# Attention's weights and maxima in steps of four heads instead of two, in a state-space convolution mixed with segmented attention

## The chip, the core and the metric

The kernel runs on one core of a Trainium2 chip. The metric is the device time of one execution in microseconds (us). Five engines of the core matter here and run side by side, each with its own queue of instructions in fixed order: TensorE (PE, with the weight loads shown apart as PEld), VectorE (DVE), ScalarE (ACT), GpSimd (POOL) and SyncE (SP), which here only issues DMAs.

## What is computed

Two branches read the same `x` of 2048 rows by 448 columns and are mixed by a gate per row. Branch A is a long convolution whose kernel is a sum of 256 damped oscillations per column; branch B is attention with 16 heads of 28 columns, in 4 segments of 512 rows, causal inside a segment, with a running memory across segments.

```python
def _A_ref(u, ...):
    P = jnp.exp((A * dt[:, None])[:, :, None] * pos[None, None, :])
    K = 2.0 * jnp.einsum("dn,dnl->dl", C, P).real
    y = jnp.fft.irfft(jnp.fft.rfft(u_t, L2) * jnp.fft.rfft(K, L2)[None], L2)[:, :, :L]
    return y + u * D_skip[None, None, :]

def _B_ref(x, wq, wk, wv, wo, beta):
    for s in range(N):                       # 4 segments of 512 rows
        logits = jnp.einsum("bhqd,bhkd->bhqk", qs, ks) * scale + mask
        a_dot = jnp.einsum("bhqk,bhkd->bhqd", _softmax(logits, axis=-1), vs)
        num = jnp.einsum("bhld,bhde->bhle", pq, M)
        den = jnp.einsum("bhld,bhd->bhl", pq, z)[..., None] + 1e-6
        outs.append(g * num / den + (1.0 - g) * a_dot)
        ...
    return o @ wo

g = _sigmoid((x * gate_w).sum(-1, keepdims=True))
return g * a + (1 - g) * b
```

## The kernel before

The work has two halves. The first (`first_half`, to about 444 us) makes the convolution's kernel and, woven into it, the projections q, k and v; q and k go to DRAM, split into a high and a low part. The change does not touch it. The second half (`second_half`, line 1206) does everything that the change touches.

**Units.** Attention is cut into 16 units: 4 segments times 4 groups of 4 heads. In SBUF the four heads of a unit lie in four blocks of 32 partitions, so that a product of one head uses 32 of TensorE's 128 rows: one row tile (`tile_position=(32 * h, 0)`). For each unit there are three steps.

- `maxima(i)` (line 974) computes the plain logits, queries by keys, and takes each row's maximum on DVE (line 994, tile `jk` with the result in `mx`). It then transposes the maxima on PE and stores them, negated, into an unused row of q by a DMA of the POOL queue (lines 1001 to 1005), so that the exponent needs no further subtraction.
- `weigh(i)` (line 1008) computes the logits again, keys by queries, in three products for each head (high by high, low by high, high by low), and ACT writes their exponentials to `PT` (line 1024). POOL then blanks the triangle above the diagonal (line 1035).
- `values(i)` (line 1037) multiplies `PT` by v on PE (tile `ps_pv`), and ACT copies the result to `pvs` (line 1055).

**Places.** Of the 512 by 512 logits of a head only the causal part is computed, in four blocks of 512, 384, 256 and 128 columns. `PLACES` (line 972) packs them into three places of one PSUM bank each: place 0 has 512 columns, place 1 has 384 and 128, place 2 has 256. In `maxima` the tile `ps_a` is written from `ku,qu`, in `weigh` from `qu,ku`.

**Steps of two heads.** `STEPS` and `MSTEPS` list six steps a unit: each place, for one half `hp` of the heads. A step takes one PSUM buffer `ps_a` of two banks, one bank for each of its two heads. The maxima of a step use the half of the heads that the weights beside it do not use.

**Three buffers.** PSUM holds three buffers `ps_a` (six of its eight banks), handed out in turn, one bank `ps_m` and one bank `ps_pv`. The convolution, the transform of its kernel and the last stage take buffers from the same three: `transform_k` two for each step (products `kb,s1k`, copied out by ACT and DVE as `gs`), `convolve` one for each step (`gk,cf`, read by ACT as `ks`; `gu,cf`, read by DVE as `pr`; `pr,cb`, read by ACT as `bs`), `finish.last` one (`bt,fc`, read by DVE).

**Order.** All products stand on PE in the order in which the program writes them. That order is written by hand in `second_half`. A first loop of 8 steps runs `transform_k` with the maxima of unit 0 and the first of unit 1 between; four more steps of unit 1 follow. Then comes a round for each unit `i`, in six turns `r`: a step of `maxima(i + 2)` (`ahead`) and a step of `weigh(i)` (`w`); at `r` 0 and 1 the tail of `maxima(i + 1)` (`behind`); at `r` 1 `values(i - 1)`; at the other turns a step of a segment's end (`seg_end`: reciprocals by way of DRAM, products `r,sel`, then four projections `wo,pvs`, 8 records each, into the one bank `ps_m`); and from round 1 to 12 some 1.15 steps of the convolution a turn. Rounds 14 and 15 have no maxima left and run `last` instead. The order on DVE and ACT is made when the program is built, from a schedule.

**Unread products.** `turn_over(n)` (line 1223) runs n products of 128x512 in bf16 into `ps_pv` that nobody reads (tile `wz`). Round 0 has three at each turn, the other rounds 1, 3 and 3 at the turns 3, 4 and 5 (`WARM`), the loop ahead of the rounds 4 times three, and the steps with `last` one each: 143 in all.

## Time and profile before

| What | us |
|---|---|
| runs of the kernel (median of 3) | 850.76 (848.26 to 857.52) |
| profiled execution, first to last instruction | 850.4 |
| transform of the convolution's kernel, maxima of units 0 and 1 | 444 to 476 |
| round 0 | 476 to 489.8 |
| rounds 1 to 12 | 489.8 to 750.8 |
| round 13 | 750.8 to 788 |
| rounds 14 and 15 | 788 to 833 |
| last projection and stores | 833 to 850.4 |

The borders of the rounds are the starts of each round's first exponential on ACT, less 1 us. The profile gives no time of its own for the profiled execution beside its span of 850.4 us; that lies 0.4 us under the median of the runs, so what is worked out against the span can be set beside the median. In the views, "idle before" with an arrow names what ended an engine's wait; `32*128 32x512` is a product on 32 rows with 512 columns, and a product in plain fp32 has two records.

### The profile page before, as it was taken

How to read it: one execution, taken by the hardware profiler on the slowest of the kernel's cores; microseconds unless marked ns; L12 is line 12 of the kernel's file. 1: busy time of each engine (PE TensorE's matmuls, PEld its weight loads, DVE VectorE, ACT ScalarE, POOL GpSimd, SP SyncE). 2: the span in 40 equal slices, each digit the busy share in tenths (PEclk: the TensorE clock that was granted, in tenths of full speed). 3: DMA queues.
4: the chain of work that ended last, by engine and by line, in shares of the span. 5: the costliest groups of instructions: out<-in, count | busy, mean ns of one | idle time of the engine just before them, and what ended most of it. 6: DMA issues, size and time to landing. Idle time of an engine off the chain costs nothing.

```text
span 850.4 us, 19021 instructions
## 1 busy us (share of the span) xinstructions
PE 750.1 (88%) x7608; PEld 405.1 (48%) x7608; DVE 582.0 (68%) x1143; ACT 538.6 (63%) x638; POOL 171.8 (20%) x217
## 2 busy tenths in 40 slices
PE   1686987998879989899988999989997998988997
PEld 1363655764546655566643444434443444343443
DVE  8878678767788676876687765656565757563474
ACT  4867889799998989898863255554453444521320
POOL 5314111011110111001110121341115113331110
PEclk9589999999999989799999899999999999979899
DMA  9347853325642346314558967667466645654872
GB/s 248 91 108 237 247 186 112 99 91 172 197 143 85 104 153 200 132 46 149 178 202 349 349 221 235 204 220 233 118 219 220 194 152 182 210 205 152 223 231 97
DMA packets 88290, 152.98 MB, mean 180 GB/s; under 512 B 20626, under 2 KB 57162, under 8 KB 88154
## 3 DMA queue, kind: packets, MB, share of 16 engines
q1 hardware_dynamic: 79130, 140.83, 51.7%
q10 hardware_dynamic: 7424, 9.18, 3.1%
q0 software_dynamic: 1648, 1.76, 0.8%
q8 instruction: 60, 0.98, 0.5%
q14 instruction: 28, 0.23, 0.1%
HBM read 90.87 MB, written 60.63 MB: 178 GB/s over the span
## 4 chain that ended last, share of the span: by engine, by line
PE 54%; ACT 16%; DVE 15%; DMA 7%; issue 6%; POOL 1%; SPq 1%; ACTq 0%; DVEq 0%; POOLq 0%
PE ps_a L1379 19%; PE ps_m L1379 17%; PE ps_pv L1379 8%; ACT cs L1344 7%; PE ps_arg L1379 5%; PE ps_k L1379 3%; DVE jk L994 3%; DVE Y L397 2%; ACT L1344 2%; PE ps_m L1382 2%; DVE Y L398 1%; DVE X L393 1%; DMA xt<-in_A_u 1%; ACT EX L1344 1%; DMA ident<-in_c_id 1%
## 5 line engine op out<-in xcount | busy, mean ns | idle before, releaser
L994 DVE CUSTOM_DVE_ANT_0 jk<-ps_a,mk 128x512 f32<-128x512 f32 (+3 forms) x256 | 124.9, 488 | 71.0 <-PE ps_a L1379 63.7
L1024 ACT ACTIVATE PT<-ps_a 128x1024 f32<-128x1024 f32 (+1 forms) x96 | 84.5, 881 | 118.6 <-PE ps_a L1379 112.0
L359 POOL TENSOR_TENSOR EX<-EX,cab 128x1024 f32<-128x1024 f32 x28 | 53.5, 1913 | 309.1 <-ACT EX L1344 244.8
L1344 ACT ACTIVATE cs<-ps_arg 128x1024 f32<-128x1024 f32 x111 | 107.3, 1021 | 0.6 <-DVE Y L398 0.3
L1379 PE MATMUL ps_m<-xh,w 112*128 112x512 f32 x256 | 92.9, 412 | 0.4 <-DVE lo L765 0.4
L1379 PE MATMUL ps_a<-qu,ku 32*128 32x512 f32 (+3 forms) x768 | 89.3, 353 | 1.7 <-DVE mx L994 1.4
L1035 POOL TENSOR_SCALAR_AFFINE_SELECT PT<-PT 128x256 f32<-128x256 f32 (+1 forms) x96 | 46.5, 485 | 206.5 <-ACT PT L1024 206.4
L393 DVE TENSOR_TENSOR X<-EX,cs 128x1024 f32<-128x1024 f32 x56 | 68.3, 1220 | 25.4 <-ACT cs L1344 25.4
L1379 PE MATMUL ps_k<-Y,X 128*32 128x64 f32 x3584 | 64.1, 226 | 9.0 <-DVE Y L398 8.8
L1379 PEld LDWEIGHTS ps_k<-Y,X 128*32 128x32 f32 x3584 | 54.9, 113 | 35.2 <-DVE Y L398 16.1
L397 DVE TENSOR_TENSOR Y<-EY,cs 128x1024 f32<-128x1024 f32 x56 | 70.0, 1250 | 0.0
L1379 PEld LDWEIGHTS ps_a<-qu,ku 32*128 32x128 f32 x768 | 62.4, 194 | 12.4 <-DVE mx L994 4.7
L1344 ACT ACTIVATE cs<-cs,bhp 128x1024 f32<-128x1024 f32 x56 | 64.5, 1151 | 1.8
L399 DVE SCALAR_TENSOR_TENSOR Y<-EY,cs 128x512 f32<-128x512 f32 x56 | 41.0, 732 | 31.2 <-ACT cs L1344 29.1
L1344 ACT ACTIVATE EY<-ps_arg 128x1024 f32<-128x1024 f32 x52 | 53.1, 1031 | 11.1 <-PE ps_arg L1379 10.1
L1379 PEld LDWEIGHTS ps_m<-xh,w 112*128 112x128 f32 x256 | 48.0, 188 | 19.7 <-issue 7.6
L1379 PE MATMUL ps_a<-ku,qu 32*128 32x512 f32 (+3 forms) x256 | 46.0, 394 | 12.3 <-DVE mx L994 9.9
L1379 PE MATMUL ps_arg<-ct,lh 64*128 64x512 bf16 x224 | 43.6, 387 | 9.0 <-ACT cs L1344 5.7
L1379 PE MATMUL ps_m<-xl,w 112*128 112x512 f32 x128 | 50.3, 393 | 0.0
L1379 PEld LDWEIGHTS ps_a<-ku,qu 32*128 32x128 f32 x256 | 22.2, 189 | 58.7 <-DVE mx L994 27.0
L1379 PEld LDWEIGHTS <-lh 64*128 64x128 bf16 x392 | 22.2, 95 | 53.4 <-issue 39.8
L606 DVE TENSOR_TENSOR pr<-ps_a,ks 128x896 f32<-128x896 f32 x32 | 34.8, 1087 | 17.7 <-PE ps_a L1379 17.0
(212 smaller groups left out, 1395.3 us busy)
## 6 DMA issues: line engine op xcount, KB each, us to landing
w<-WD SPq DMA_DIRECT2D x32, 448.0 KB, 4.7
qu<-QD SPq DMA_DIRECT2D x16, 512.0 KB
ku<-KD SPq DMA_DIRECT2D x16, 512.0 KB
GU<-gs SPq DMA_DIRECT2D x32, 224.0 KB, 2.5
GK<-gs SPq DMA_DIRECT2D x8, 896.0 KB, 5.1
gk<-GK SPq DMA_DIRECT2D x32, 224.0 KB, 4.7
gu<-GU SPq DMA_DIRECT2D x32, 224.0 KB, 3.7
BB<-bs ACTq DMA_DIRECT2D x16, 448.0 KB, 2.6
```

Of the source, the lines that this page charges most:

```text
L359: nc.gpsimd.tensor_tensor(o, o, cab, ALU.mult)
L393: v.tensor_tensor(X, ex, t[:, :, 0], ALU.mult)
L397: v.tensor_tensor(Y[:, :, :, :32], lo, y[:, :, :, ::-1], ALU.mult)
L398: v.tensor_tensor(Y[:, 0, :, 32:], ey[:, :, 32:], y[:, 0], ALU.mult)
L399: v.scalar_tensor_tensor(Y[:, 1, :, 32:], ey[:, :, 32:], -1.0, y[:, 1], ALU.mult, ALU.mult)
L606: nc.vector.tensor_tensor(pr[c], pt, ks.pop(c), ALU.mult)
L994: v.tensor_tensor_reduce(junk[:, :n], pt[:, x, o : o + n], k.mk[:, SEG - n :], 1.0, -3e38, ALU.add, ALU.max, mx[:, 3 - t, h : h + 1],)
L1024: nc.scalar.activation(PT[:, 2 * hp : 2 * hp + 2, 512 * b : 512 * b + n], pt[:, :, :n], AF.Exp, scale=SCALE)
L1035: nc.gpsimd.affine_select(sl, sl, pat, ALU.is_ge, 0.0, base=0, channel_multiplier=-1)
L1344: x = op(*args, **kw)
L1379: tc.keep_in_program_order(nc.tensor.matmul(*args, **kw))
L1382: tc.keep_in_program_order(nc.tensor.transpose(*args))
```

## The change

`weigh` and `maxima` no longer work on two heads in a step but on four: a step takes two `ps_a` buffers and issues, for its place, the products of all four heads, one head on each row tile. A unit then has three steps of weights and three of maxima instead of six and six. In the rounds they go by turns: the weights at `r` 0, 2 and 4, the maxima of the unit two ahead at `r` 1, 3 and 5. The list of maxima on the other half of the heads (`MSTEPS`) goes, and so do the unread products of rounds 1 to 15 (`WARM`); those of round 0 and of `last` stay, and of the loop ahead of the rounds two of the four remain, since that loop has two steps instead of four. Everything else, each product's size and number and all DMAs, is as before.

```diff
-    STEPS = [(b, hp) for b in range(3) for hp in range(2)]
-    MSTEPS = [(b, 1 - hp) for b, hp in STEPS]
...
     def maxima(i):
-        for b, hp in MSTEPS:
-            pt = k.ps("a")
-            for t, o, n in PLACES[b]:
+        for place in PLACES:
+            pts = [k.ps("a") for _ in range(2)]
+            for t, o, n in place:
                 qt = 3 - t
-                for x in range(2):
-                    h = 2 * hp + x
+                for h in range(4):
                     r = slice(32 * h, 32 * h + 32)
                     k.mm(
-                        pt[:, x, o : o + n], q[r, 0, 128 * qt : 128 * qt + 128], kk[r, 0, :n],
+                        pts[h // 2][:, h % 2, o : o + n], q[r, 0, 128 * qt : 128 * qt + 128], kk[r, 0, :n],
...
     def weigh(i):
-        for b, hp in STEPS:
-            pt = k.ps("a")
-            for kt, o, n in PLACES[b]:
+        for b, place in enumerate(PLACES):
+            pts = [k.ps("a") for _ in range(2)]
+            for kt, o, n in place:
                 for a, (x, y) in enumerate(((0, 0), (1, 0), (0, 1))):
-                    for z in range(2):
-                        h = 2 * hp + z
+                    for h in range(4):
...
-        for _ in range((0, 1, 2, 1, 2, 1, 1, 0)[r]):
+        if r in (1, 2, 4, 5, 6):
             step(ms[0])
-        if r >= 6:
+        if r == 7:
             step(ms[1])
...
-    for r in range(4):
+    for r in range(2):
         turn_over(3)
         step(ms[1])
...
             if i == 0:
                 turn_over(3)
-                step(w)
-                step(ahead)
-            else:
-                if r in WARM:
-                    turn_over(WARM[r])
-                step(ahead)
-                step(w)
+            step(ahead if r % 2 else w)
...
-WARM = {3: 1, 4: 3, 5: 3}
```

How the products stand on PE in the middle of a plain round, before (round 2, from its place 1 on). `gk,cf` and `gu,cf` are the convolution's, `ku,qu` the maxima's, `qu,ku` the weights':

```order
L1379 MATMUL ps_a<-gk,cf 128x448 x2
L1379 MATMUL ps_a<-ku,qu 128x384 x2
L1379 MATMUL ps_a<-ku,qu 128x128 x2
L1379 MATMUL ps_a<-qu,ku 128x384 x6
L1379 MATMUL ps_a<-qu,ku 128x128 x6
L1379 MATMUL ps_a<-gu,cf 128x448 x2
L1379 LDWEIGHTS wz
L1379 MATMUL ps_pv<-wz 128x512
L1379 MATMUL ps_a<-ku,qu 128x384 x2
L1379 MATMUL ps_a<-ku,qu 128x128 x2
L1379 MATMUL ps_a<-qu,ku 128x384 x6
L1379 MATMUL ps_a<-qu,ku 128x128 x6
```

And after (round 3, the same place and the one behind it):

```order
L1369 MATMUL ps_a<-gu,cf 128x448 x2
L1369 MATMUL ps_a<-gk,cf 128x448 x2
L1369 MATMUL ps_a<-qu,ku 128x384 x12
L1369 MATMUL ps_a<-qu,ku 128x128 x12
L1369 MATMUL ps_a<-gu,cf 128x448 x2
L1369 MATMUL ps_a<-ku,qu 128x384 x4
L1369 MATMUL ps_a<-ku,qu 128x128 x4
L1369 MATMUL ps_a<-pr,cb 64x448 x4
L1369 MATMUL ps_a<-qu,ku 128x256 x12
L1369 MATMUL ps_a<-gk,cf 128x448 x2
L1369 MATMUL ps_a<-ku,qu 128x256 x4
L1369 MATMUL ps_a<-gu,cf 128x448 x2
```

The maxima moved away from the weights that stood right behind them, by one or two steps of the convolution, and the unread products between the steps are gone.

On DVE the reductions of a place stand in one run of four heads. Of the same stretch before, one place of two heads, then another, with the convolution's `pr` between:

```order
L994 ISA jk,mx<-ps_a,mk 128x384
L994 ISA mx 128x1
L994 ISA jk,mx<-ps_a,mk 128x128
L994 ISA mx 128x1
L994 ISA jk,mx<-ps_a,mk 128x128
L994 ISA mx 128x1
L606 TENSOR_TENSOR pr<-ps_a,ks 128x896
L994 ISA jk,mx<-ps_a,mk 128x384
L994 ISA mx 128x1
L994 ISA jk,mx<-ps_a,mk 128x384
```

And after:

```order
L606 TENSOR_TENSOR pr<-ps_a,ks 128x896 x2
L991 ISA jk,mx<-ps_a,mk 128x384
L991 ISA mx 128x1
L991 ISA jk,mx<-ps_a,mk 128x384
L991 ISA mx 128x1
L991 ISA jk,mx<-ps_a,mk 128x128
L991 ISA mx 128x1
L991 ISA jk,mx<-ps_a,mk 128x128
L991 ISA mx 128x1
L991 ISA jk,mx<-ps_a,mk 128x384
L991 ISA mx 128x1
```

Two of `pr` moved together ahead of the place, and the eight reductions of a place 1 follow one another.

In the last rounds PE has the weights beside `last` (`bt,fc`), before (round 15):

```order
L1379 MATMUL ps_a<-bt,fc 64x448 x4
L1379 LDWEIGHTS wz
L1379 MATMUL ps_pv<-wz 128x512
L1379 MATMUL ps_a<-qu,ku 128x384 x6
L1379 MATMUL ps_a<-qu,ku 128x128 x6
L1379 MATMUL ps_a<-bt,fc 64x448 x4
L1379 LDWEIGHTS wz
L1379 MATMUL ps_pv<-wz 128x512
L1379 LDWEIGHTS wz
L1379 MATMUL ps_pv<-wz 128x512
L1379 MATMUL ps_a<-qu,ku 128x384 x6
L1379 MATMUL ps_a<-qu,ku 128x128 x6
```

And after:

```order
L1369 MATMUL ps_a<-bt,fc 64x448 x4
L1369 LDWEIGHTS wz
L1369 MATMUL ps_pv<-wz 128x512
L1369 MATMUL ps_a<-qu,ku 128x384 x12
L1369 MATMUL ps_a<-qu,ku 128x128 x12
L1369 MATMUL ps_a<-bt,fc 64x448 x4
L1369 LDWEIGHTS wz
L1369 MATMUL ps_pv<-wz 128x512
L1369 MATMUL ps_m<-pvs,den 128x512
```

Here the two bursts of weights became one, and one unread product a step is left. (The line numbers of the changed file are 3 lower inside `attend` and 10 lower behind `second_half`.)

28 lines of the change are left out of this document (15 added, 13 removed).

## Prediction

> **What bounds the kernel now.** I read the stages first, then the chain of waits inside a round, then single rows. One execution by stage (the columns are length, busy time of PE, PEld, DVE, ACT and POOL, granted PE clock, share of the DMA engines, GB/s):
>
> ```profile
> 476.00:489.80 13.80, 13.25 (x87) 6.82 (x87) 8.84 (x36) 5.79 (x7) 2.85 (x7) 0.75 0.97 350
> 489.80:542.30 52.50, 51.36 (x417) 23.42 (x415) 31.82 (x107) 29.94 (x36) 10.58 (x22) 1.00 0.67 208
> 542.30:615.20 72.90, 68.66 (x465) 30.37 (x464) 41.22 (x123) 32.57 (x40) 19.50 (x34) 0.98 0.62 201
> 615.20:633.70 18.50, 18.50 (x150) 8.60 (x152) 11.83 (x37) 10.31 (x13) 3.82 (x8) 1.00 0.63 202
> 633.70:750.80 117.10, 106.77 (x739) 47.88 (x733) 71.60 (x204) 51.87 (x64) 38.68 (x61) 0.94 0.57 187
> 788.00:833.00 45.00, 44.72 (x279) 18.45 (x279) 26.08 (x37) 12.56 (x16) 7.04 (x14) 0.93 0.80 226
> ```
>
> In the plain rounds 1 to 3 and 7 (second and fourth row; 17.5 us each on average, and 18.5) PE is busy all the time, DVE and ACT some 60%. The chain of waits over round 7 stays on PE almost wholly, a fifth of it in the bank `ps_pv`, where the unread products go too:
>
> ```profile
> by line: PE ps_a L1379 71.8%; PE ps_pv L1379 21.7%; ACT bs L619 4.9%; PE ps_m L1382 2.8%; PE ps_m L1379 1.2%; issue 0.1%
> ```
>
> So these rounds are PE's own length. They are also well packed:
>
> ```profile
> 586.05 1.02 PE L1379 MATMUL ps_a<-gk,cf 64*128 64x448 f32 x4
> 587.01 0.50 PE L1379 MATMUL ps_a<-ku,qu 32*128 32x512 f32 x2
> 587.01 0.96 PE L1379 MATMUL ps_a<-qu,ku 32*128 32x512 f32 x6
> 587.90 1.40 PE L1379 MATMUL ps_m<-wo,pvs 128*128 128x448 f32 x3
> ```
>
> Two products of the maxima start in the same 10 ns as the first two of the weights, because they use the other two row tiles, and all eight give way to the next work after 0.89 us: the time of the six alone. Before the change the maxima are nearly free on PE, and four row tiles already work at once for a third of the time.
>
> **The change, part by part.**
>
> *Four heads in a burst.* Twelve products on four tiles are not in this trace, so I bound them: 0.89 us if four tiles take the time of two, 1.78 us if not. The nearest row is the convolution kernel's transform, on four tiles:
>
> ```profile
> 451.19 2.00 PE L1379 MATMUL ps_a<-kb,s1k 32*128 32x448 f32 x16
> ```
>
> 16 records of 448 columns in 2.00 us with the tail is four at a time; I take 0.89, and 1.1 and 0.6 for places 1 and 2. The maxima now stand alone and pay for themselves, about 0.4 us a burst. A round then has 2.6 + 1.2 = 3.8 us of these products against 2 x 2.6 = 5.2 before, a gain of 1.4 us of PE (a loss of 1.2 at the other end).
>
> *Unread products.* Three take 0.75 us of PE's time, start to next start:
>
> ```profile
> 578.14 0.82 PE L1379 MATMUL ps_pv<-wz 128*128 128x512 bf16 x3
> 578.89 0.38 PE L1379 MATMUL ps_a<-ku,qu 32*128 32x256 f32 x2
> ```
>
> Seven in a round go, 1.8 us; with the loop ahead it is 111 of 143. So PE's own work in a plain round falls from 17.5 to about 14.3 us. What it waits for next are the buffers.
>
> *Two buffers a step, of three.* The durations that decide (ACT's exponential of two heads, DVE's reductions of one head by place, the convolution's readers):
>
> ```profile
> L1024 ACT ACTIVATE PT<-ps_a 128x1024 f32<-128x1024 f32 x64 | 65.4, 1024 | 73.9 <-PE ps_a L1379 67.3 <-ACT bs L619 3.2 <-DMA gk<-GK 1.1
> L994 DVE CUSTOM_DVE_ANT_0 jk<-ps_a,mk 128x512 f32<-128x512 f32 x64 | 44.0, 687 | 14.6 <-PE ps_a L1379 13.2
> L994 DVE CUSTOM_DVE_ANT_0 jk<-ps_a,mk 128x384 f32<-128x384 f32 x64 | 35.5, 554 | 30.1 <-PE ps_a L1379 28.4
> L606 DVE TENSOR_TENSOR pr<-ps_a,ks 128x896 f32<-128x896 f32 x32 | 34.8, 1087 | 17.7 <-PE ps_a L1379 17.0
> L601 ACT ACTIVATE ks<-ps_a 128x896 f32<-128x896 f32 x32 | 29.3, 917 | 13.6 <-PE ps_a L1379 13.1 <-PE ps_pv L1379 0.5
> L994 DVE CUSTOM_DVE_ANT_0 jk<-ps_a,mk 128x256 f32<-128x256 f32 x64 | 27.0, 422 | 24.3 <-PE ps_a L1379 22.1 <-DVE mx L994 0.5
> L994 DVE CUSTOM_DVE_ANT_0 jk<-ps_a,mk 128x128 f32<-128x128 f32 x64 | 18.4, 288 | 2.0
> ```
>
> ```profile
> 634.75 1.02 ACT L1024 ACTIVATE PT<-ps_a 128x1024 f32<-128x1024 f32 x1 [0.50 <-ACT bs L619]
> 635.79 0.69 DVE L994 CUSTOM_DVE_ANT_0 jk<-ps_a,mk 128x512 f32<-128x512 f32 x1 [0.60 <-PE ps_a L1379]
> 635.82 0.53 PEld L1379 LDWEIGHTS ps_a<-qu,ku 32*128 32x128 f32 x6 [0.38 <-ACT PT L1024]
> 636.53 0.69 DVE L994 CUSTOM_DVE_ANT_0 jk<-ps_a,mk 128x512 f32<-128x512 f32 x1
> 636.71 2.36 PE L1379 MATMUL ps_pv<-PT,V 128*32 128x512 f32 x32
> ```
>
> Here ACT's read ends at 635.77 and the next weights on that buffer start at 635.82: a buffer comes back 0.05 us after its reader. One reduction follows another after 0.74 us, so four of place 0 take 3.0 us, the eight of place 1 3.8, the four of place 2 1.9. With these I walk through round 3 in the changed order (time 0 at its first weights; the buffers in turn x, y, z; `gk` and `gu` 0.96 us each, as from 586.05 to 587.01; `pr,cb` 1.65; values, the row of 2.36 us, with four transposes 2.8). Weights 0 (x, y) leave PE at 0.9; ACT reads x until 2.1 and y until 3.0. `gk` fills 0.9 to 1.9. The maxima need x and y: two heads go at 2.1, two at 3.1. DVE reduces from 2.7 to 5.7. Values, transposes, `gu` and `gk` keep PE going until 8.2. Weights 1 (y, z) wait for `pr` on z until 8.45 and end at 9.5; `gu` to 10.45. Maxima 1 wait for ACT, two heads at 10.65, two at 11.6, and DVE has them until 15.4. `pr,cb` ends at 13.75. Weights 2 need both halves of those maxima and wait until 15.4. `gk`, maxima 2 and `gu` then lose another 0.9 to ACT, and the next round's weights come at 19.4. PE works 14.1 us of these and waits 5.3; the largest wait, 1.7 us, is for DVE, which is nowhere the bound before. 19.4 against 17.5: the gain on PE is more than given back. Walked in the same way, a round with one convolution step in every gap comes to 18.8, and one where `pr` stands ahead of the last reduction of place 1 to 20.4. I take 19.6, +2 us for each of the four plain rounds: **+8**.
>
> *Rounds 4 to 6 and 8 to 12* hold the segments' ends too, four projections per segment and some broadcasts, one at a turn:
>
> ```profile
> 773.34 3.27 PE L1379 MATMUL ps_m<-wo,pvs 128*128 128x448 f32 x8
> ```
>
> These fill gaps of 1 to 1.7 us, so much of the waiting hides behind them and the saved PE work shows. If all hid, each round would win 1.6 us (-13); if none, each would lose 2 (+16). I take **-4**. Round 13, bound by projections through one bank: 0.
>
> *Ahead of the rounds.* Each transform step takes two buffers, and now each maxima step too, so DVE must finish half a place before the next transform, and ACT and DVE must copy before the next maxima. Before, the first maxima start at 451.18, held by a DMA:
>
> ```profile
> 451.18 0.50 PE L1379 MATMUL ps_a<-ku,qu 32*128 32x512 f32 x2 [1.97 <-DMA ku<-KD]
> 476.04 0.96 PE L1379 MATMUL ps_a<-qu,ku 32*128 32x512 f32 x6 [0.84 <-DVE mx L994]
> ```
>
> Walked through in the same way from 451.2, the first weights come at 482.5 instead of 476.0. Round 0 has no convolution, so its two-buffer steps overlap over three buffers; it takes 12.1 us against 13.8. Together **+5**.
>
> *Rounds 14 and 15* have no maxima, so the weights run on two tiles alone, and PE is full:
>
> ```profile
> 799.40 1.08 PE L1379 MATMUL ps_a<-qu,ku 32*128 32x384 f32 x12
> 800.41 1.72 PE L1379 MATMUL ps_a<-bt,fc 128*64 128x448 f32 x8
> 802.07 1.25 PE L1379 MATMUL ps_pv<-wz 128*128 128x512 bf16 x4
> 803.25 0.62 PE L1379 MATMUL ps_a<-qu,ku 32*128 32x256 f32 x6
> ```
>
> Half of some 8 us of weights and 14 unread products (0.25 each) go: -7.5, of which the DMA share of 0.80 in the stage row above lets perhaps **-5** through.
>
> *The clock.* PE's granted clock falls to half for a window of 3.41 us where PE was idle too long in the one before:
>
> ```profile
> 555.70:559.10 3.40, 1.74 (x15) 0.63 (x11) 3.35 (x12) 0.38 (x1) 3.40 (x4) 1.00 1.01 369
> 559.10:562.50 3.40, 3.02 (x9) 0.79 (x7) 1.13 (x5) 1.51 (x2) 2.16 (x4) 0.50 0.19 47
> 644.40:647.80 3.40, 1.95 (x13) 0.61 (x9) 1.63 (x8) 1.02 (x1) 1.67 (x2) 1.00 1.05 385
> 647.80:651.30 3.50, 1.34 (x12) 0.76 (x14) 3.47 (x9) 0.60 (x1) 3.49 (x5) 0.99 0.36 131
> ```
>
> 1.74 us of 3.4 was followed by half clock (0.50), 1.95 not (0.99). In a cold window `pr,cb` took 2.64 us:
>
> ```profile
> 631.56 1.72 PE L1379 MATMUL ps_a<-pr,cb 128*64 128x448 f32 x8
> 650.58 2.64 PE L1379 MATMUL ps_a<-pr,cb 128*64 128x448 f32 x8 [1.29 <-DVE pr L606]
> 653.14 1.76 PE L1379 MATMUL ps_a<-gk,cf 64*128 64x448 f32 x4
> ```
>
> That and `gk` (0.7 more) cost 1.6 us. Rounds 1 to 12 now have about five such windows (granted clock 0.98 of 72.9 us and 0.94 of 117.1 us). Without unread products and with the waits around maxima 1 and weights 2 I expect ten: **+8**. The ends are 0 and, with two in every round, +30.
>
> On this point the Trainium skill ("TensorE: Matmul & The Clock Gate", section "Why this matters for your kernels") asks only that there be no PE-idle gaps above about 3 us between bursts. By it the worked round would keep its clock and the sum would be 8 us less, 855. The trace does not agree: the longest gap ahead of the cold window at 559.1 was 1.66 us (`DVE mx`).
>
> Nothing changes in the DMAs: the store of the maxima on POOL's queue still goes out at turn 1, a whole round ahead of its reader. The sum is 8 - 4 + 5 - 5 + 8 = +12 on a span of 850.4; the median of the runs lies 0.4 above the span, so **863 us**.
>
> **The rivals.**
>
> *The clock swings in every round.* If the waits are longer than walked, half of each round runs cold: one window more in each of 12 rounds at 1.7 us is +20, 883 us. For it: no margin at 1.74 to 1.95. Against it: a cold PE is busier and so recovers. The same page, section "A second HAM failure mode: psum-queue depth-cycling", describes this swing for kernels that pause at PSUM buffers.
>
> *The waits hide, and PE's saving stays* (faster). The place is the gap behind maxima 1: with two convolution steps or a projection there, weights 2 find their buffers free. It decides when the waits of a plain round stay under 3.2 us, the PE work saved. With 2.4 us left, 4 x -0.8, -13 in the other eight rounds, +5, -5 and no more cold windows give -16: 835 us.
>
> *It comes out even.* The waits are as walked, but the clock keeps to its five windows and the eight rounds hide more: +8 - 13 + 5 - 5 + 4 = -1, 850 us.
>
> **How the numbers follow.** A run tells about 1% (842 to 859) from no change. My forecast has 0.50, with a range of its own of 855 to 873 (0.10 of it under 859); the swinging clock 0.20; even 0.18; the hidden waits 0.12 (0.09 of it under 842). So faster 0.09, the same 0.10 + 0.18 + 0.03 = 0.31, slower 0.40 + 0.20 = 0.60. The range of 845 to 882 leaves out most of the hidden waits and half of the swinging clock; a serial burst of four heads (+2.6 us a round against what I took) lies above it.
>
> **What would show it.** Right: in the changed profile twelve products of place 0 leave PE in about 0.9 us; maxima products are in two pairs about 1 us apart, the second released by ACT `PT`; weights 2 wait for `DVE mx` by 1 us or more; plain rounds take 19 to 21 us; the first weights come near 482; rounds 14 and 15 are some 5 us shorter. Wrong: PE still above 95% busy in rounds 1 to 3, or fewer half-clock windows than before.

## The result, and the profile after

The changed kernel takes 893.08 us (median of 4 runs, 882.54 to 899.15) against 851.25 us before on the same chip (848.26 to 857.52): a ratio of 1.0426, with a 95% interval of 1.0365 to 1.0488. The change makes the kernel some 4% slower. The highest of the four runs, 899.15 us, fell in the chip's slower state and is not in the ratio. The forecast was 863 us with a range of 845 to 882; the direction was right, the size (12 us of 42) less than a third of what was measured.

The profiled execution of the changed kernel is the shortest of its runs: span 880.8 us, 30.4 us over the 850.4 us of before. So the profile can explain 30 us. The two other runs in the ratio take 10 and 11 us more; no trace shows where, and that part stays open.

The stages again, by the same borders (length, busy time of PE, PEld, DVE, ACT and POOL, granted PE clock, share of the DMA engines, GB/s). The rows are round 0, rounds 1 to 3, 4 to 6, 7, 8 to 12, 13, and rounds 14 and 15 with the end; the last row is rounds 1 to 12 together:

```profile
479.00:492.10 13.10, 11.06 (x82) 4.91 (x83) 7.71 (x31) 5.55 (x7) 3.43 (x7) 0.81 1.06 389
492.10:556.80 64.70, 53.32 (x392) 22.82 (x392) 32.40 (x108) 28.97 (x36) 10.25 (x21) 0.84 0.51 162
556.80:636.20 79.40, 66.83 (x443) 28.62 (x447) 42.80 (x125) 32.40 (x41) 19.58 (x33) 0.88 0.57 187
636.20:661.20 25.00, 20.16 (x144) 8.47 (x143) 11.64 (x36) 9.14 (x12) 3.44 (x7) 0.77 0.44 151
661.20:791.10 129.90, 101.33 (x702) 43.29 (x698) 73.87 (x203) 49.83 (x64) 39.68 (x61) 0.84 0.49 162
791.10:822.30 31.20, 23.46 (x142) 11.54 (x142) 18.68 (x48) 8.81 (x13) 5.22 (x9) 0.94 0.66 243
822.30:880.80 58.50, 49.05 (x306) 19.80 (x302) 34.31 (x49) 12.20 (x16) 6.70 (x13) 0.91 0.71 198
492.10:791.10 299.00, 241.65 (x1670) 103.20 (x1674) 160.71 (x471) 120.34 (x152) 72.95 (x122) 0.85 0.51 168
```

Three things changed in the plain rounds 1 to 3 and 7: they are longer (64.7 for 52.5 us, 25.0 for 18.5), PE is busy 82 and 81% of them and not 98 and 100%, and its clock, which was 1.00, is 0.84 and 0.77. The chain of waits over rounds 1 to 3 has gone from PE to a mixture:

```profile
by line: PE ps_a L1369 35.8%; DVE jk L991 12.4%; issue 8.8%; PE ps_pv L1369 7.1%; ACT PT L1021 6.4%; DVE pr L606 5.1%; PE ps_m L1372 1.6%; DVE mx L991 0.7%; DVEq L991 0.1%; DVEq L606 0.1%
```

What PE waited for at `ps_a` in rounds 1 to 12 (total, times, longest):

```profile
PE ps_a L1369 <- DVE mx L991: 23.2, 15, 5.9
...
PE ps_a L1369 <- DVE pr L606: 19.0, 13, 4.3
...
PE ps_a L1369 <- ACT PT L1021: 7.2, 16, 1.0
...
PE ps_a L1369 <- ACT ks L601: 5.5, 10, 1.1
```

The kernel before has only two of these lines above half a microsecond in its rounds 1 to 12:

```profile
PE ps_a L1379 <- DVE mx L994: 10.5, 11, 3.5
PE ps_a L1379 <- DVE pr L606: 2.9, 6, 1.3
```

Nearly all of the waits after the change are for a reader to give a buffer back. The exception is 6.8 of the 19.0 us for `pr`: they stand ahead of `pr,cb`, which reads `pr` itself. One wait for a buffer in full, weights 2 of round 2, on PE and on DVE:

```profile
526.78 0.38 PE L1369 MATMUL ps_a<-qu,ku 32*128 32x256 f32 x2 [0.94 <-DVE mx L991]
528.76 1.01 PE L1369 MATMUL ps_a<-qu,ku 32*128 32x256 f32 x10 [1.60 <-DVE mx L991]
```

```profile
527.47 0.56 DVE L991 CUSTOM_DVE_ANT_0 jk<-ps_a,mk 128x384 f32<-128x384 f32 x1
...
528.07 0.29 DVE L991 CUSTOM_DVE_ANT_0 jk<-ps_a,mk 128x128 f32<-128x128 f32 x1
...
528.40 0.29 DVE L991 CUSTOM_DVE_ANT_0 jk<-ps_a,mk 128x128 f32<-128x128 f32 x1
528.62 0.08 DVE L991 DVE_READ_ACCUMULATOR2_ANT mx<- 128x1 f32 x1
```

The first two heads of the weights start after 0.94 us; the other two need the second buffer, on which DVE still reduces the maxima of place 1. Its last read ends at 528.70, and PE goes on at 528.76.

Not every wait for `DVE mx` is time spent on reductions. The longest of them, 5.91 us in round 8, shows what else holds DVE; first PE's row, then DVE's:

```profile
679.21 0.58 PE L1369 MATMUL ps_a<-qu,ku 32*128 32x256 f32 x2 [5.91 <-DVE mx L991]
```

```profile
674.84 0.55 DVE L1061 RECIPROCAL rc<-dn 128x64 f32<-128x64 f32 x1 [5.20 <-DMA dn<-pvs]
...
677.34 0.55 DVE L991 CUSTOM_DVE_ANT_0 jk<-ps_a,mk 128x384 f32<-128x384 f32 x1
```

The reductions stand in DVE's queue behind the reciprocal of a segment's end, and that waits for a DMA. Three of PE's waits for `DVE mx`, 11.3 of the 23.2 us, have such work of a segment's end in front of the reductions. The kernel before has waits of this kind too (2.31 us at 648.66).

And what such waits do to the clock, in the stretches of 3.4 us around the two of round 2 (columns as above):

```profile
521.50:524.90 3.40, 2.84 (x38) 1.59 (x34) 1.10 (x2) 2.76 (x3) 1.19 (x3) 1.00 0.89 276
524.90:528.30 3.40, 1.33 (x6) 0.40 (x6) 3.08 (x14) 0.92 (x1) 0.00 (x0) 1.00 0.74 231
528.30:531.70 3.40, 2.94 (x18) 1.43 (x18) 0.39 (x5) 1.09 (x2) 1.23 (x2) 0.50 0.23 64
531.70:535.10 3.40, 2.65 (x10) 0.85 (x12) 2.71 (x9) 0.00 (x0) 0.00 (x0) 0.50 0.81 312
535.10:538.50 3.40, 3.40 (x19) 1.34 (x16) 0.00 (x0) 1.66 (x2) 0.00 (x0) 0.50 0.31 99
538.50:541.90 3.40, 3.15 (x28) 1.05 (x28) 2.15 (x7) 2.01 (x3) 0.82 (x2) 0.99 0.59 185
```

PE is busy 1.33 us of a stretch and the next is at half clock. Busy 2.94 and 2.65 us there does not bring the clock back; it returns only after a stretch that is busy throughout. These two waits, 0.94 and 1.60 us one behind the other, cost three stretches of half clock.

**A sum that can be compared.** For rounds 1 to 12 I split each kernel's length into PE's work at full clock, PE's waits (length less PE's busy time) and what the half clock adds (half of PE's busy time inside the half-clock stretches, added up record by record; the row of `pr,cb` at 532.82 takes 3.25 us there, 1.72 at full clock). Rounds are cut 1 us ahead of the first exponential on ACT. Since some matmul records are missing, the split between work and waits is good to about 5 us. Rounds 1 to 12 before, beside the last row of the stages above:

```profile
489.80:750.80 261.00, 245.28 (x1756) 110.27 (x1754) 156.48 (x470) 124.68 (x152) 72.58 (x123) 0.97 0.61 196
```

| Rounds 1 to 12, us | length | work | waits | half clock adds | time at half clock |
|---|---|---|---|---|---|
| before | 261 | 238 | 16 | 8 | 17 |
| after | 299 | 208 | 57 | 34 | 92 |

So 29 us of PE's work did go; the waits gave back 42, and the half clock took 26 more. Outside these rounds little moved: round 1 begins 2.3 us later, round 13 is 6.0 us shorter (31.2 for 37.2), rounds 14 and 15 with the end 3.9 us shorter (58.5 for 62.4).

### The profile page after: what moved, and what is told of

Read it like the earlier page. It is cut to its first block, busy times and chain, and to the rows that moved or that the text cites. A ratio compares the mean times of both kernels' runs of the same rounds, so it can differ in the third digit from the quotient of the medians.

```text
span 880.8 us, 18786 instructions
## 1 busy us (share of the span) xinstructions
PE 728.6 (83%) x7490; PEld 387.5 (44%) x7497; DVE 587.3 (67%) x1143; ACT 532.8 (60%) x638; POOL 172.1 (20%) x217
## 5 line engine op out<-in xcount | busy, mean ns | idle before, releaser
L991 DVE CUSTOM_DVE_ANT_0 jk<-ps_a,mk 128x512 f32<-128x512 f32 (+3 forms) x256 | 125.4, 490 | 56.3 <-PE ps_a L1369 44.1
L1021 ACT ACTIVATE PT<-ps_a 128x1024 f32<-128x1024 f32 (+1 forms) x96 | 79.4, 879 | 113.3 <-PE ps_a L1369 112.1
L1369 PE MATMUL ps_a<-qu,ku 32*128 32x384 f32 (+3 forms) x768 | 61.9, 393 | 36.4 <-DVE mx L991 24.1
L1369 PEld LDWEIGHTS ps_a<-qu,ku 32*128 32x128 f32 x768 | 40.4, 213 | 75.0 <-DVE mx L991 47.3
L1369 PE MATMUL ps_a<-ku,qu 32*128 32x512 f32 (+3 forms) x256 | 36.3, 427 | 12.5 <-ACT PT L1021 6.7
L1369 PE MATMUL ps_a<-gu,cf 64*128 64x448 f32 x128 | 38.5, 684 | 6.5 <-ACT ks L601 4.9
```

The source lines that it names most:

```text
L991: v.tensor_tensor_reduce(junk[:, :n], pts[hp][:, x, o : o + n], k.mk[:, SEG - n :], 1.0, -3e38, ALU.add, ALU.max, mx[:, 3 - t, h : h + 1],)
L1021: nc.scalar.activation(PT[:, 2 * hp : 2 * hp + 2, 512 * b : 512 * b + n], pts[hp][:, :, :n], AF.Exp, scale=SCALE)
L1369: tc.keep_in_program_order(nc.tensor.matmul(*args, **kw))
```

## The experiments

Two theories stood at the start. *A*: the clock. Without unread products PE has too little to do, falls to half clock, and that is the loss. *B*: the buffers. A step that takes two of the three buffers makes the next work wait for DVE and ACT; the clock only follows. Ratios are to the kernel before in the same batch; the changed kernel's is 1.0426.

**Three unread products at five of the six turns of rounds 1 to 15 in the changed kernel**, and **none in these rounds of the kernel before**:

```diff
+            elif r in WARM:
+                turn_over(WARM[r])
...
+WARM = {0: 3, 1: 3, 3: 3, 4: 3, 5: 3}
```

> The changed kernel with three unread products put back ahead of the step at turns 0, 1, 3, 4 and 5 of the rounds 1 to 15 (11 us of PE work in all 15 rounds would be 15 x 15 x 0.25 = 56 us if none of it fell into waits). Theory A (the clock): of the 30 us that the profile lost, some 15 are waits for PSUM buffers and the rest is half clock, 27 cold windows in rounds 1 to 12 against 5. Then the fillers run inside the waits, the cold windows fall under 10, and the time comes to 860 to 875. Theory B (buffers alone): the waits carry the whole loss and the clock only follows; then fillers give back nothing, 885 to 900, whatever the clock shows. Were they a pure cost, 900 to 940.

```diff
-WARM = {3: 1, 4: 3, 5: 3}
+WARM = {}
```

> The kernel before with the unread products of rounds 1 to 15 taken out and nothing else (steps of two heads stay). Theory A: its steps leave PE shorter pauses than the changed kernel's, but some windows fall below the gate: 8 to 15 cold windows in rounds 1 to 12 instead of 5, and 850 to 865. Theory B: the fillers were plain PE work on a PE-bound path; without them 825 to 842.

The first: 894.74 us, ratio 1.0471 (1.0420 to 1.0521). Time at half clock fell from 92 to 52 us, and nothing was won: PE has 38 us more work (246 us). The second: 850.01 us, ratio 0.9918 (0.9872 to 0.9963), a little faster than before. Its rounds 1 to 12, one row:

```profile
485.00:748.70 263.70, 231.83 (x1672) 108.17 (x1671) 157.28 (x470) 124.34 (x152) 72.68 (x123) 0.93 0.60 197
```

Work 218, waits 32, half clock 14. The rounds are nearly as long as with the unread products (263.7 for 261.0), with 19 us less work, 16 us more waits and 6 us more from the clock. So the unread products were not what the change lost. From here this kernel, steps of two heads without unread products, is the one to compare with: against it the change has 10 us less work, 25 us more waits and 20 us more from the clock.

**Weights and maxima on the same half of the heads**, in the kernel before:

```diff
-    MSTEPS = [(b, 1 - hp) for b, hp in STEPS]
+    MSTEPS = STEPS
```

> The kernel before with the maxima on the same half of the heads as the weights beside them, so that they share two row tiles and must follow one another. If the pairing on four tiles is what made the maxima nearly free, each step's burst grows from 0.89 to about 1.15 us, 6 steps x 0.2 to 0.3 us x 14 rounds = +17 to +25 us, 866 to 878. If the maxima hide in waits anyway: within 4 us of before.

858.54 us, ratio 1.0044 (1.0002 to 1.0087); the work in rounds 1 to 12 rose from 238 to 246 us. That the maxima of two heads run beside the weights of the other two was worth some 4 us (0 to 7 by the interval). The change gave this up, but that is about a tenth of its loss.

**The tail alone**: the weights of rounds 14 and 15 in steps of four heads, without unread products there, in the kernel before.

```diff
+        if i >= 14:
+            for b, place in enumerate(PLACES):
+                pts = [k.ps("a") for _ in range(2)]
...
+            elif i >= 14:
+                if r % 2 == 0:
+                    step(w)
```

> The kernel before, with steps of four heads in rounds 14 and 15 alone, where there are no maxima, and without the unread products of those two rounds but those beside the last stage. If the four-tile burst is worth there what the stage after shows (58.6 us for rounds 14, 15 and the end against 62.3, with more cold time): -4 to -7 us, 844 to 848, less than before. If the stage is held by its DMAs: within 2 us.

851.30 us, ratio 0.9974 (0.9937 to 1.0010): unclear. PE gets through the weights earlier and then meets a load of the last stage:

```profile
818.88 2.14 PE L1400 MATMUL ps_a<-bt,fc 128*64 128x448 f32 x8 [3.60 <-DMA bt<-BB]
```

**Unread products only at the waits** of the changed kernel, and the **reductions cut to 64 columns**:

```diff
+            elif i < 14 and r in WARM:
+                turn_over(WARM[r])
...
+WARM = {0: 2, 4: 8, 5: 2}
```

> The changed kernel with unread products only where the trace of it shows PE waiting: two ahead of the weights of places 0 and 2 (turns 0 and 5) and eight ahead of the last weights (turn 4) of rounds 1 to 13. Theory A (clock: PE has too little to do in many windows, and the half clock is what costs): the cold time of rounds 1 to 12, 92 us in the changed kernel, falls to below 50 us, and since the unread products stand in waits, the time falls with it by about 1 us for each cold window of 3.4 us won, to 870 to 880 us. Theory B (the two buffers of a step make the next work wait, and the clock is an effect of it): unread products only fill time that is waited anyway, or push the queue back where the waits do not stand; time 888 to 900 us whatever the clock does.

```diff
-                            junk[:, :n], pts[hp][:, x, o : o + n], k.mk[:, SEG - n :], 1.0, -3e38,
+                            junk[:, :64], pts[hp][:, x, o : o + 64], k.mk[:, SEG - n : SEG - n + 64], 1.0, -3e38,
```

> The changed kernel with each reduction of the maxima on VectorE over the first 64 columns of its block only; this leaves out most of the maxima's reductions, and the products on PE stay. VectorE then gives a step's buffers back early. Theory B (the chain is: a step of four heads takes two of the three buffers, the next step waits until VectorE has read both): the waits of the weights for the maxima's reductions, 46.5 us in rounds 1 to 12, go to below 10 us, plain rounds fall from 20 to 25 us to 16 to 18 us, and the time to 835 to 855 us. Theory A (too few products on PE for the clock, whoever reads the buffers): the cold windows stay at 20 or more in rounds 1 to 12 and the time at 870 us or above. If VectorE is not what the buffers wait for but ScalarE's exponentials (33.0 us of waits), the time lies between, 860 to 875 us.

The first: 883.10 us, ratio 1.0334 (1.0284 to 1.0383). Rounds 1 to 3 of it are wholly at full clock and still 60.3 us long, 8 more than in the kernel with steps of two heads:

```profile
497.30:557.60 60.30, 54.34 (x427) 22.62 (x428) 32.44 (x108) 28.97 (x36) 10.21 (x21) 1.00 0.56 181
```

So theory A, with the unread products that it calls for, wins about 1 of the 4 per cent. The second: 860.27 us, ratio 1.0080 (1.0044 to 1.0116), 3.5 points less than the changed kernel. PE's waits for the reductions fell from 23.2 to 17.9 us and PEld's from 46.5 to 0.3 us; rounds 1 to 12 still spend 71 us at half clock. The time came out between the numbers of both theories, in the range set down for waits on ScalarE's exponentials, and those stayed as they were (7.5 us on PE against 7.2). Of the 17.9 us left for `DVE mx`, three waits at segments' ends are 10.8. So DVE's reductions are a large part of the cause, not all.

**Two heads after two**: the changed kernel's steps, with all products of heads 0 and 1 ahead of those of heads 2 and 3.

```diff
+            for hp in range(2):
...
-                    for h in range(4):
+                        for h in (2 * hp, 2 * hp + 1):
```

> The changed kernel with the same steps, by turns, and the same two buffers for each step, but the products of heads 0 and 1 of a place all stand ahead of those of heads 2 and 3, as in the kernel before: two row tiles at work instead of four. The first buffer is complete after half of the step's products, so its exponential or its reductions start earlier, but the step's products take as long as before the change. Theory B (buffers): the earlier start of the first reader shortens the waits by some 0.5 us a step and PE loses some 0.9 us of pairing at most, so the time stays within 1% of the changed kernel, 884 to 902 us; the order by turns and the two buffers cost the 43 us. Theory C (the burst on four row tiles itself costs, since readers get both buffers at once): 860 to 875 us.

885.64 us, ratio 1.0365 (1.0294 to 1.0436); its interval overlaps the changed kernel's. Four tiles at once are neither the loss nor, here, a gain.

**Both together** on the kernel before: no unread products in rounds 1 to 13, the tail in steps of four, and six buffers instead of five for one of the last stage's loads (five instead of six for the other), so that these loads start a step earlier.

```diff
-        bts[wc] = fp.tile([128, 2, 2, D], F32, tag="bt", name="bt", bufs=5)
+        bts[wc] = fp.tile([128, 2, 2, D], F32, tag="bt", name="bt", bufs=6)
...
-WARM = {3: 1, 4: 3, 5: 3}
+WARM = {}
```

> The kernel before without unread products in rounds 1 to 13 and with the weights of rounds 14 and 15 in steps of four heads, and with six buffers instead of five for the loads of the last stage (and five instead of six for its other operand), so that the last stage's loads start one step earlier. Without the unread products alone the ratio was 0.9918; with the tail alone 0.9974, where 3.6 us of the tail's 5 us went to a wait for one load of the last stage. If the two add up, and the wait for the load goes: 838 to 845 us, ratio 0.986 to 0.990. If the load waits as before: 845 to 850 us.

851.40 us, ratio 0.9959 (0.9928 to 0.9990). The wait for the load is gone from the profile, yet the time is not below that of the kernel without unread products alone. The tail is worth nothing that can be measured.

**Each half of the change alone**, without unread products: the maxima in steps of four and the weights in steps of two, and the reverse.

```diff
+            if r % 2:
+                step(ahead)
+            step(w)
```

> The changed kernel with the weights back in six steps of two heads, one a turn; only the maxima stay in steps of four heads at the turns 1, 3 and 5, and there are no unread products. Theory B1 (what costs is that two steps of two buffers each follow one another with one step of the convolution between, so that a step's first buffer is wanted about 1 us after the last step filled it): here a step of one buffer always stands between, plain rounds fall to 17 to 18.5 us and the time to 843 to 858 us. Theory B2 (VectorE takes some 3 us for the four reductions of a step, and that alone costs, whatever follows): rounds stay at 19 us and above and the time at 865 to 880 us.

```diff
+            step(ahead)
+            if r % 2 == 0:
+                step(w)
```

> The kernel before with the weights in steps of four heads at the turns 0, 2 and 4; the maxima stay in six steps of two heads, one a turn, ahead of the weights, and there are no unread products in rounds 1 to 15. Theory B1 (two steps of two buffers in a row): no such pair here, time 838 to 855 us. Theory B2 (VectorE's four reductions in one step): none here either, 838 to 850 us. Theory B3 (the weights' burst of four heads, which needs two buffers and fills them for ScalarE at once, costs by itself): plain rounds of 19 us and more, 862 to 880 us. With the kernel that has only the maxima in steps of four heads this tells which half of the change costs.

The maxima alone: 917.44 us, ratio 1.0717 (1.0625 to 1.0809), worse than both together. The weights alone: 883.67 us, 1.0334 (1.0268 to 1.0400). Both expectations B1 fell: I had said that a step of one buffer between two steps of two would mend it. The first lies above every range that I had set down; the second, 4 us above the range of B3, in which the weights' two buffers cost by themselves. Rows of PE in the first show how the waits arise:

```profile
526.14 0.50 PE L1373 MATMUL ps_a<-ku,qu 32*128 32x384 f32 x4
527.24 1.07 PE L1373 MATMUL ps_a<-qu,ku 32*128 32x384 f32 x12 [0.60 <-DVE pr L606]
528.98 1.02 PE L1373 MATMUL ps_a<-gk,cf 64*128 64x448 f32 x4 [0.67 <-DVE mx L993]
530.96 1.01 PE L1373 MATMUL ps_a<-qu,ku 32*128 32x256 f32 x6 [0.95 <-DVE mx L993]
531.90 1.87 PE L1373 MATMUL ps_a<-gu,cf 64*128 64x448 f32 x4
533.70 0.59 PE L1373 MATMUL ps_a<-ku,qu 32*128 32x256 f32 x4
535.03 1.01 PE L1373 MATMUL ps_a<-qu,ku 32*128 32x256 f32 x6 [0.74 <-DVE pr L606]
```

The maxima take two buffers in half a microsecond. The weights behind them get the third, which the convolution filled just before, and wait for its reader (`pr`, whose read takes 1.09 us); the convolution gets the maxima's first, the next weights their second. Each is asked for one short step after it was filled. The waits come to 46 us in rounds 1 to 12, less than in the changed kernel, but 48 of the 56 are shorter than 1 us, where the changed kernel has 17 of 58 longer. The time at half clock is 126 us, which adds 56 us of length. That the even spread is what keeps the clock down fits these numbers; no run tests it by itself.

**Unread products at the waits and short reductions together**, and **short reductions in the kernel before** as control, without unread products:

```diff
+                            junk[:, :64], pts[hp][:, x, o : o + 64], k.mk[:, SEG - n : SEG - n + 64], 1.0, -3e38,
...
+WARM = {0: 2, 4: 8, 5: 2}
```

> The changed kernel with both of two earlier edits: reductions over 64 columns only (this leaves out most of the maxima's reductions) and unread products at the waits. Apart they won 3.4 and 0.9 per cent of the changed kernel. If the clock and the reductions are two causes that add up: 848 to 855 us, with fewer than ten cold windows in rounds 1 to 12. If the clock's swings were only the shadow of the waits for VectorE: the unread products win nothing more or cost, 858 to 868 us. Plain rounds that stay above 18 us at full clock would show that a third part, the waits of the weights' second buffer for ScalarE, is still there.

```diff
+                        junk[:, :64], pt[:, x, o : o + 64], k.mk[:, SEG - n : SEG - n + 64], 1.0, -3e38,
...
+WARM = {}
```

> The kernel before without unread products in rounds 1 to 15 and with reductions over 64 columns only (this leaves out most of the maxima's reductions). It is the control for the same edit on the changed kernel, which won 3.4 per cent there. If VectorE's reductions bound only the steps of four heads, the time here stays within 1% of the same kernel with whole reductions: 835 to 850 us. If they are worth as much in steps of two heads (10 us or more), the 3.4 per cent is not the change's: below 832 us.

The first: 858.94 us, ratio 1.0062 (1.0024 to 1.0100), level with short reductions alone, though time at half clock fell from 71 to 27 us: the unread products cost what the clock wins. Rounds 1 to 3 take 19.8 us each at a clock of 0.97, over the 18 us that I had named as the sign that waits for ScalarE's exponentials remain. The control: 842.50 us, 0.9861 (0.9812 to 0.9911), 0.6 points below whole reductions. So some 2.9 of the 3.5 points are the change's own.

**A fourth buffer** for all four forms. The banks `ps_m` and `ps_pv` go, and their users take the first bank of one of four shared buffers:

```diff
+            if tag not in shapes:
+                return p.tile(shapes["a"][0], F32, tag="a", name="ps_" + tag, bufs=4)[:, 0]
...
-            {"m": ([128, 512], 1), "a": ([128, 2, 512], 3), "pv": ([128, 512], 1)},
+            {"a": ([128, 2, 512], 4)},
```

> The changed kernel with four buffers ps_a of two banks instead of three: the single banks ps_m and ps_pv go, and their users take the first bank of one of the four. Buffers as the cause: PE's waits in rounds 1 to 12 fall from 57 us to 40 us or less, the half clock follows them, from 92 us to 50 us or less, and the time falls to 850 to 868 us. Lumps that the readers have to work off as the cause: waits and clock stay, 878 to 895 us.

> The control: the kernel before without unread products in rounds 1 to 15, with the same four shared buffers. If three were enough for steps of one buffer: within 1% of the same kernel with three, 834 to 850 us. If it wins 10 us or more, a fourth buffer helps any form and is no test of the change.

> The kernel with only the weights in steps of four heads, with four shared buffers. With three it had a ratio of 1.0334, 48 us of waits and 65 us of half clock in rounds 1 to 12. Buffers as the cause: 840 to 856 us, waits below 38 us. Otherwise 872 to 885 us.

> The kernel with only the maxima in steps of four heads, with four shared buffers. With three it had a ratio of 1.0717, 46 us of waits and 126 us of half clock in rounds 1 to 12. Buffers as the cause: 850 to 875 us, half clock below 60 us. Otherwise 900 to 918 us.

| Steps of four heads in | three buffers | four buffers |
|---|---|---|
| neither (no unread products) | 0.9918 (0.9872 to 0.9963) | 0.9795 (0.9713 to 0.9877) |
| weights | 1.0334 (1.0268 to 1.0400) | 0.9849 (0.9801 to 0.9896) |
| maxima | 1.0717 (1.0625 to 1.0809) | 1.0124 (1.0055 to 1.0193) |
| both (the change) | 1.0426 (1.0365 to 1.0488) | 1.0104 (1.0061 to 1.0147) |

The fourth buffer wins 1.2 points without the change, 3.2 to 5.9 with it. All times lay in the ranges that buffers as the cause would give, though the control's gain is some 10 us, just the mark at which I had said that a fourth buffer helps any form; what speaks for the buffers is that the other forms gain about three to five times as much. The weights' half of the change now costs 0.5 points and no longer 4.2. The path was not wholly as expected, though: in the changed kernel PE's waits fell from 57 to 46 us only (40 expected), and the time at half clock stayed at 88 us (50 expected); with the maxima alone in steps of four it fell from 126 to 68 us (60 expected). PE's waits by reader in the changed kernel with the fourth buffer:

```profile
PE ps_a L1369 <- DVE mx L991: 24.0, 15, 6.0
...
PE ps_a L1369 <- DVE pr L606: 8.8, 6, 3.1
...
PE ps_a L1369 <- ACT PT L1021: 4.3, 10, 1.0
```

Those for `pr` and for the exponentials fell (19.0 and 7.2 with three buffers), those for the reductions did not (23.2). Three waits at segments' ends, where DVE still waits for its DMA, are 13.4 of the 24.0 us (11.3 with three). What was left between the forms, 3.1 points, sits in the maxima's half.

**What is left with four buffers**: short reductions, or unread products at the waits.

```diff
+                            junk[:, :64], pts[hp][:, x, o : o + 64], k.mk[:, SEG - n : SEG - n + 64], 1.0, -3e38,
...
+            {"a": ([128, 2, 512], 4)},
```

> The changed kernel with four shared buffers and with reductions over 64 columns only (this leaves out most of the maxima's reductions). If the rest is VectorE's lump: waits in rounds 1 to 12 below 35 us, 832 to 846 us, level with the kernel before in the same two edits or nearly so. If the rest is the half clock by itself or ScalarE's exponentials: 850 to 862 us.

```diff
+WARM = {0: 2, 4: 8, 5: 2}
...
+            {"a": ([128, 2, 512], 4)},
```

> The changed kernel with four shared buffers and with unread products at the waits (two ahead of the weights of places 0 and 2, eight ahead of the last weights, rounds 1 to 13). If the half clock by itself is the rest: cold time below 35 us in rounds 1 to 12 and 838 to 852 us. If the clock only follows the waits: the products cost what the clock wins, 856 to 870 us.

The first: 834.21 us, ratio 0.9733 (0.9655 to 0.9811); PE's waits for the reductions are halved, and of the 12.2 us left three waits at segments' ends are 11.1; all of PE's waits come to 39 us, where I expected less than 35. Rounds 1 to 3 are at full clock with nothing added for it:

```profile
PE ps_a L1369 <- DVE mx L991: 12.2, 7, 4.7
```

```profile
484.80:533.40 48.60, 43.74 (x400) 19.82 (x396) 19.25 (x111) 28.81 (x36) 11.03 (x23) 1.00 0.81 254
```

The second: 861.45 us, 1.0104 (1.0062 to 1.0145), the same ratio as without them, with the time at half clock down from 88 to 26 us. So the half clock by itself is not the rest. The lump of reductions that a step of four heads hands to DVE is what remains as its cause, with the clock behind it; that this lump costs only the steps of four heads is not shown with four buffers, since steps of two were not run with both edits.

The splits of rounds 1 to 12, as above:

| Rounds 1 to 12, us | length | work | waits | half clock adds | time at half clock |
|---|---|---|---|---|---|
| steps of two, no unread products | 264 | 218 | 32 | 14 | 36 |
| changed, unread products at the waits | 293 | 243 | 38 | 12 | 31 |
| changed, short reductions | 283 | 208 | 47 | 28 | 71 |
| maxima alone in steps of four | 328 | 227 | 46 | 56 | 126 |
| weights alone in steps of four | 289 | 213 | 48 | 28 | 65 |
| changed, four buffers | 283 | 203 | 46 | 34 | 88 |
| changed, four buffers, short reductions | 263 | 204 | 39 | 19 | 50 |
| weights alone in steps of four, four buffers | 268 | 207 | 37 | 24 | 55 |
| maxima alone in steps of four, four buffers | 283 | 219 | 34 | 30 | 68 |
| steps of two, no unread products, four buffers | 264 | 217 | 26 | 21 | 48 |

The last of these is also the best kernel that leaves none of the reductions out: 839.87 us, ratio 0.9795, faster than both the kernel before and the changed one. It has the unread products taken away, as the change does, and keeps the steps of two heads.

## Why the prediction was wrong

**Right: the burst and, in the main, PE's saving.** Rows of PE in the changed kernel show 24 products of place 1, and 12 of place 0, on four tiles:

```profile
499.28 1.08 PE L1369 MATMUL ps_a<-qu,ku 32*128 32x384 f32 x24
...
844.10 0.97 PE L1369 MATMUL ps_a<-qu,ku 32*128 32x512 f32 x12
```

They take the time that half as many took on two tiles (1.08 and 0.96 us), as I had assumed. PE's work at full clock fell by 2.2 us a round in rounds 1 to 3 and by 3.0 in round 7, where 3.2 was forecast.

**Right in kind: the walk through a plain round.** The maxima come in pairs, the second held by ACT, and weights 2 wait for `DVE mx` by 0.94 and 1.60 us (one wait of 1.7 forecast). At full clock rounds 1 to 3 would take 56.3 us, 18.8 each (19.6 taken), and the four plain rounds together 5.6 us more than before: the term was +8. Round 3, the one of rounds 1 to 3 with little half clock (1.8 us), took 20.0 us. As measured, with the half clock, they take 21.6 and 25.0 us, where 19 to 21 was to be the sign. And DVE was not "nowhere the bound before": PE waited 10.5 us for `DVE mx` in rounds 1 to 12 then.

**Wrong: "The clock ... I expect ten: +8".** This is the step that failed most. Rounds 1 to 12 have 92 us at half clock, 27 stretches of 3.41 us where I expected ten and before had five; they add 34 us instead of 8, 26 more. The price of a stretch was well taken (1.2 us measured, 1.6 forecast); the number was not: the prediction has no count of stretches behind its ten, and it read a threshold between 1.74 and 1.95 us busy out of two stretches, where one busy 2.28 us also lost the clock (last section). Its own far end, +30, covered the 26 us measured. The argument against the rival, that "a cold PE is busier and so recovers", was false here. It is busier, 2.65 to 2.94 us of 3.4 above, and does not recover. The rival "the clock swings in every round" named the right mechanism, and its 883 us is nearest. The Trainium skill ("TensorE: Matmul & The Clock Gate", section "A second HAM failure mode: psum-queue depth-cycling") describes this swing for a PE that idles briefly again and again between its groups of products while it cycles through PSUM; the trace agrees, with 27 half-clock stretches in ten spells over 299 us.

**Wrong: rounds 4 to 6 and 8 to 12, -4.** At full clock they cost 7 us more than before: some 20 us of saved work against 27 us of new waits. The projections cover fewer waits than I thought, because a wait sits inside a step, between its first two heads and the other two, where nothing else can stand: four such waits of 2.07 to 2.15 us for `pr` fall in these rounds. The value lies in the bounds that I gave (-13 to +16), on the other side of zero.

**Small terms.** Round 1 begins 2.3 us later (+5 forecast). But the first half, which the change does not touch, ended 2.0 us earlier in this execution (first `kb,s1k` at 442.7 for 444.7), so from there to round 1 it is 4.3 us; the first weights came at 477.7, not at 482. Round 13: -6.0 (0 forecast), as it spent 3.9 us at half clock instead of 13.9. Rounds 14 and 15: -3.9 (-5 forecast). With 5.6 and 7 us of the rounds at full clock and 26 us of the clock, that is 31 us beside the 30.4 us between the spans. Of the rivals, the one that comes out even adds +4 for a clock that is said to keep its five windows; without that its sum is 846 us.

**What lies beneath.** I treated the waits and the clock as separate terms. The experiments point to one main cause with two prices. The cause is how soon a buffer is wanted again after it was filled: with a fourth buffer the difference between the forms falls from 5.1 to 3.1 points, and with short reductions on three buffers from 5.1 to 2.2; with both at once the changed kernel is at 0.9733, below the forms in steps of two with either edit alone (0.9795 and 0.9861), though the intervals overlap. The clock by itself, bought back with unread products, was worth 0.9 points with three buffers and nothing with four. The control of both edits in steps of two was not run, so whether the four-head step itself then wins is left open. Beside this cause stand PE's waits at the segments' ends, 11 to 13 us for `DVE mx` in all four of these forms of the changed kernel, which neither edit takes away.

## What to carry to other kernels

Before packing a step more tightly on PE, count after how much other work each PSUM buffer is wanted again, and compare that with how long its reader holds it; a step that takes two buffers of three leaves one use of another buffer in between instead of two, and one half of such a change can be worse than the whole. Count half clock not by the wait but by the stretch: a short wait can cost several, because in most cases the half clock lasted until PE had been busy for nearly a whole stretch. Filling waits with unread products moved the loss here from the clock into PE's own work; more buffers, or shorter holds, took part of it away (2.0 and 2.9 of 5.1 points). And where a wait names a reader, look at what stands ahead of it in its queue.

## What the runs showed of the hardware

- **The clock has a hysteresis:** how busy PE must be to win full clock back is more than it needs to keep it. Over the stretches of 3.41 us between 444 and 790 us in all twenty profiled executions: from full clock, PE busy below 45% was followed by half clock in 80 of 80, above 85% in none of 1122, in between in 105 of 439. From half clock, PE busy below 75% stayed there in 90 of 90, 75 to 95% in 64 of 78, above 95% in 49 of 220. These counts are made from the records, of which some are missing.
- **No long gap is needed.** The stretch ahead of the half clock at 504.4 has PE busy 2.28 of 3.40 us, and the longest wait of PE in or at its end is 0.94 us; first its row among the stretches, then PE's rows in it:

```profile
501.00:504.40 3.40, 2.28 (x16) 0.78 (x12) 2.52 (x7) 1.85 (x3) 0.81 (x2) 1.00 0.35 108
```

```profile
502.38 0.50 PE L1369 MATMUL ps_a<-ku,qu 32*128 32x384 f32 x6 [0.47 <-ACT PT L1021]
...
504.77 0.58 PE L1369 MATMUL ps_a<-qu,ku 32*128 32x256 f32 x2 [0.94 <-DVE mx L991]
```

The Trainium skill ("TensorE: Matmul & The Clock Gate", section "Why this matters for your kernels") asks for no PE-idle gap above about 3 us; by that rule this stretch keeps its clock, and the measurement decides against it.

- **Half of a change can cost more than the whole.** The maxima alone in steps of four heads were 2.9 points slower than maxima and weights together, with fewer waits (46 against 57 us) and more time at half clock (126 against 92 us).
